# Attention and a SwiGLU block in one program: the same 1027 tasks, planned anew (order, engines, PSUM banks)

## The chip, the cores and the metric

The kernel runs on one core of a Trainium2 chip. That core has five engines with an instruction queue each: PE (TensorE, the matmuls), ACT (ScalarE), DVE (VectorE), POOL (GpSimd) and SP (SyncE, which here only issues DMAs). Each queue runs in its written order, and an engine waits where the next instruction's inputs or its buffer are not ready. The metric is the device time of one execution in microseconds (us), as a median over runs.

## The reference

```python
# q, k, v: 4 batches x 8 heads x 768 tokens x 64
scores = np.matmul(q, k.T) / np.sqrt(64)
causal  = rel >= 0                              # rel = query position - key position
stream  = causal & (key < 4 | rel < 64)         # 4 sink tokens and a window of 64
mask    = causal for heads 0, 2 and 6, stream for the other five
a       = softmax(where(mask, scores, -1e9))
x       = (a @ v) laid out as 3072 tokens x 512
g, val  = x @ w_gate, x @ w_val                 # 512 -> 1536
out     = (g * sigmoid(g) * val) @ w_out        # 1536 -> 512, float32
```

## The kernel before

All matmuls are in fp16 with float32 sums in PSUM. The 3072 queries are cut into 24 **tiles** of 128; two neighbouring tiles are a **pair** (0 to 11), and four tiles a **group** (0 to 5) of 512 tokens, on which the feed-forward part works. Everything is written as 1027 named **tasks**, each with its inputs, the engines on which it may run, and the buffers it takes:

- `load q3`, `load k3`, `load x3` (x is v) and `load g0`, `v0`, `o0` (pieces of the three weight matrices): DMAs on SP, L342 to L355, into a ring of 14 raw buffers.
- `cq3`, `ck3`, `cx3.m.j`, `wc g0`: casts to fp16 on ACT, DVE or POOL (L205, L207, L211).
- q and k turned so that the head dimension lies on the partitions: for pairs 0 to 4 by PE (`trq`, `trk`, L448, evacuated by `evq`, `evk`), for pairs 5 to 11 by DMA transposes on SP (`dq5.0` and so on, L438).
- `sc8.1`: score matmuls of tile 8, unit 1 (L542). `ex8.1`: the exponential on ACT (L554). `mask8.1`: a product with a 0/1 mask on DVE or POOL (L562), for tiles from 4 on; earlier tiles have the mask added by matmuls. `val8.1`, `val8.0`: a @ v for odd and even heads (L572). `nm8`: the softmax division on DVE (L579, L580), which writes the tile of x.
- `sk`, `sv`: copies of the sink tokens' keys and values to where the window's blocks find them.
- x turned: for tiles 0 to 7 by PE (`xtr`, L596, and `xe`), from tile 8 on by a DMA transpose on SP (`xdma8`, L590).
- per group g and slice j of 128 of the 1536 columns: `gate` and `vals` on PE (both L734, four matmuls of 512 columns; group 0 has its first slices in halves, `gate0.3.256`), `tanh` on ACT (L740), `stt1` and `stt2` on DVE (L744, L751), which make silu(g)·val, the buffer `h`. `gate` and `vals` hold a PSUM bank each until `stt1` and `stt2` have read it.
- `out2.3.0` to `.2`: the out projection of group 2, tile 3 in thirds (L769); `oe2.3.0` its evacuation on ACT or DVE (L205, L207); `st2.3.0` its store, issued by SP or ACT (L787).
- 22 filler matmuls on an identity (L314) at the start: 10 in the task `warm`, 12 between other tasks.

PSUM has eight banks. `gv` and `o` buffers take one bank, `big` ones (scores, and a @ v) two. So the order of tasks on PE, and which bank each takes, decide what a matmul must wait for: its inputs, and the last reader of its bank.

The order is written out as tables. `ORDER` has two base-62 digits for each task's number, in the order in which instructions are issued; numbers from 3700 on are filler matmuls. `WAYS` has a digit for each task: which of its allowed engines. `SLOTS` has a digit for each buffer that a task takes: which place of the ring, or which bank.

```python
        for t, w in zip(self.tasks, WAYS):
            t.way = t.ways[int(w)]
...
        ENG[task().way].tensor_tensor(out=ev, in0=ev, in1=mm, op=ALU.mult)      # L562
...
        eng = nc.scalar if T_st[g, tt, x].way == "ACT" else nc.sync              # L786
        eng.dma_start(out=out[r0:r0 + 128, lo:hi], in_=o_sbs[g, tt][:, lo:hi])
...
    for number in P.order():
        if number < P.FILL:
            running.append(P.tasks[number])
            P.tasks[number].run()
        else:
            warm((number - P.FILL) % 16, (number - P.FILL) // 16)
```

Each engine runs its share of `ORDER` in that order. Work of later tiles is woven into the feed-forward part of earlier groups: scores of tile 19, for example, stand among the gates of group 3.

Of the kernel before, what the change touches and what calls it, by code (L numbers as in the profile page):

```python
# [13 lines left out]


ORDER = (
    "00070306090A0C01041K1L08xy1T1I1Jy01Q1R1o1p0D1U1SyH1w1V1W0B1x1q0h1f1r1y1X0n02xh1z2K1g1d2021221k1e"
    "1O2B1N0E232Q1P292C1M2R0g2L2S1h2A1Y1Z2G1i1a1t2T1s1u0m1v1j24251b2U2D262E2V2W0i1c2X2Z2F272h132a282c"
    "0G1m2I1n2d142l2J2r2m052o0l8r2Y912s2b2O8w2n2w940F2P8s928z8t2N8p938x0z8u2M8y0o0y8m908c958n118h1l8o"
    "0r8S108q8d8X8v8i8k168e8f8j0k8T8a8Y8U2p8V8g31968Z0J8l8W9B971F8b2q2e0H9C2f98392i9D309a0q2g3A9f9b3B"  # L20
    "172t9g9c2u0I362v9E1G372x0j3F3I3G9F9d1C9h3J0p9i3H383C9e3K3D9V0Q3j9j9Q3L3P3E329W0x343b9R9X3T33993c"
    "9S1D3U3r0P9A3M3i3N3s3V3W0u3Z3t3X9Y19353a3o3O9T3Q0t3p3Y1A9Z3u3x3v9G0w9U3q3y9L3w0M9H2j3R3z2y9M3d9I"
    "3e3S9N9O2k553f2z549J529P2H453g483h4E18404FA95141AdAA58A7ABAeATAf0sAC0vAU0O49AgAD0K15AO0LAVAhARAP"
    "0R4A1EAn53AQA4Ao1B0SASAJA51HAp12AM9K59AKAEA6AWA83m0VALAH3kAN3n9kAF3l4M9lAXAG4S9mAIAY9n4TAiAZ4N5U"
    "AsAa0N50Av4UAtAu4B424C4V6643Aw9p4JAj4D9q57469r449o4GAk9s4Q4H56Al4R4I4K4PAx0ZAm5b4ZAy4W4e4j9u4aAz"
    "5T479v4X4b4O9w0c4f4Y9t4p9x4u4L4q4c9z4v4rA05a4dA15Z4mA24s4g4h0U4tAq4i4kA34nAbAr4l4o5HAc5A5I5K0TB2"
    "0d5BB06E5C4w4xB19yB36o7E6lB44y6nB75L5XB54z5WB8655JB96CBCBA6B7o5QBDBBBE7G5MBtBFBG5d5j5g5k0YBv5e0b"
    "C30W5h5fBq5cBw5iCA5YBxBr0aBgCBBs6DBMBuBhCCByBiBNC0Bz5NBO5OCD5P6869BPC167CE5R5oBlC2C5C4Bm7CBWC65D"
    "BQ5EBjBnBUC7BX5F5VBZ6kBk5G5u5r5vBYBoBa5S5sC85wBp625lC95m6s5t6L5p5x6MBb6r5n5yBeBc5z0X60Bd5qBR63Bf"
    "CF61BS7IBHBTCGBVBI647DBJ6jCHCI7LBK7HBL6I6FCJ6N7K6JCoCK6G6K0fCL6p6O6HCp6SCMCq6qDXCNCj7JDYD8DZCk0e"  # L30
    "DaClD9DBDb73DA6t7470DCDN6u75DG79DOCy7pDP6P6QCz7wCr716RD1Cs6U72D06Y6d6ZDQD26eDD6a6TDR6V6vDE7SD66W"
    "DFD3DH6X6mCeD4CPD5CfD7CQCgCR76CS776w6x787AChCT6yCt6A7T7B7rCi6bCu7P7M7u6cCwCv7QCm7vCO7RDSCx6fCnDT"
    "6g7NCUDU6hCV7O6iCWCZCX7X7t7FCaCY6zCb7UCc7VB6DV7WCd7g7xDW7a7h7dE47bEL7e7cEJEM7fEOENE1EPEGE2EfE3E5"
    "EiEgEHEkEhEIDIElEKEBDJEmDLDKECEp7ZDMDcEDEqEj7YDdEr7lDeDhDf7i7jEn7k7m84Eo7y7n8581Di8B7zDj8280Dm83"
    "DnDkDo7q868E878HDr8IDs8F8JDt8KDu8M88898NEd8A8CEV8G8L8DEQEWEEEXER7sEYEFEsESEZ8O8PEtDw8QDzDx8RE6Dy"
    "E9DvE7EaE8EAETEbFJEcEeFsFKEUFEFtFLFWFuDpG2E0DqFTDgFiFUFFFHFVDlFXFlFjFnFkFmFqFoEuFpFrG3FMFGGAFIG7"
    "FNG4FYG8FxG9FZGBFbFyFaG0FcFRFzG5G1FOG6FvFPFgFwFQEvFSEwEzExF0EyFdGCFeF1FfFhF4F2F5F3F6F9FAFBGDFCGE"
    "FDF7GHGFF8GIGGGJGMGKGNGLGOGRGPGSGQGTGWGUGVGXGY"
)
WAYS = (  # L40
    "000000000000000000000000000000000000000000000000000000000000222202202222222202220100222201100000"
    "000000000000220020220220011011000000000000000100220222011000000000000001201000000000002001222221"
    "001001000001000000001010000000000000002201000010010000000000020000000000000020202222000000000000"
    "000001100010000000000012012200000000000001001000020220220000000100000000100001001000002200222020"
    "000000000000000001000000000000000200200000000100000010000000101110210000001000000001200000000000"
    "021020200200000010000000000020000001000000000000000000000000000000000000000000000000000000000000"
    "000000000000000000000000000000000000000001000010000000000000000000000000000000000000000000000000"
    "000000000000000100001100000000010000000000000000000000000000000000000000000000000000000000000001"
    "100001000000001000000000000000000000000000000000000000000000000000000000000000010000110001000010"
    "000000000000000000000000000000000000000000000000000000000000000000000000000000010000000000000000"  # L50
    "0000000000000000000000000000000000000000000000001000100001000001010"
)
SLOTS = (
    "010523746A20796974080CAB6C17B52493D18B8DA51C93B8452163D10106040102241611232063220254440040006220"
    "616201436425612211161624043604454120646214300622320400616445611240622523226261404460404562163226"
    "113612440602263216220446045226106560612261024342246160132543246012162406142236445612242206143605"
    "0023111440102212311231000040220111550227010245020E1113A11049001182013501026302102104125F1004B212"
    "4I3021G3111D1000H0001M4112C1020K2010L2120J1121N0110024000104502081005A11046310472024E51010001511"
    "1243311152025211109021000124000M1011K1000G1120J4105I5120H0121F4001D302280020C4000L2122B300112025"
    "1149401142003201221002260123N5022541137510033104A111101004E122012010115M3002D2004C1012G5000H1110"  # L60
    "L4011J2014K5123B2103I301080104F300112001"
)
DIGITS = "0123456789ABCDEFGHIJKLMNOPQRSTUVWXYZabcdefghijklmnopqrstuvwxyz"

# [820 lines left out]
```

## Time and profile before

| | |
|---|---|
| time, median of 3 runs | 252.2 us (251.61 to 252.58) |
| the profiled execution's own time | 250.21 us |
| its span in the profile | 248.3 us |
| PE busy | 240.2 us, 97% |
| DVE, ACT, POOL busy | 165.7, 140.1, 84.7 us |
| DMA moved | 40.69 MB, mean 164 GB/s |
| instructions | 5187 |

The span runs from the first to the last instruction that the profiler recorded on the core; 1.9 us of that execution's time lie around it. Busy is the time in which an engine has an instruction in work, which for PE includes matmuls that are issued and still wait. A row of the timeline gives start and length in us, engine, line, operation, and in square brackets how long the engine had been idle and what released it. `SPq` is SP's queue issuing a DMA, and `DMA xt<-xb` the transfer itself. In the rows by source line, three numbers with slashes are the shortest, the median and the longest instruction in ns.

### The profile page before, as it was taken

How to read it: one execution, taken by the hardware profiler on the slowest of the kernel's cores; microseconds unless marked ns; L12 is line 12 of the kernel's file. 1: busy time of each engine (PE TensorE's matmuls, PEld its weight loads, DVE VectorE, ACT ScalarE, POOL GpSimd, SP SyncE). 2: the span in 40 equal slices, each digit the busy share in tenths (PEclk: the TensorE clock that was granted, in tenths of full speed). 3: DMA queues.
4: the chain of work that ended last, by engine and by line, in shares of the span. 5: the costliest groups of instructions: out<-in, count | busy, mean ns of one | idle time of the engine just before them, and what ended most of it. 6: DMA issues, size and time to landing. Idle time of an engine off the chain costs nothing.

```text
span 248.3 us, 5187 instructions
## 1 busy us (share of the span) xinstructions
PE 240.2 (97%) x2010; PEld 126.3 (51%) x2010; DVE 165.7 (67%) x294; ACT 140.1 (56%) x219; POOL 84.7 (34%) x114
## 2 busy tenths in 40 slices
PE   7999999999999999899999999999999999999995
PEld 2667765654444564444544545544455544444443
DVE  2579899967988654299886787546843767873111
ACT  3699778887674665656855765444544634231120
POOL 7578968760343444910510092310034000000000
PEclk9999999999999999999999999999999999999999
DMA  6999999958999999992598312460110223001142
GB/s 190 357 334 340 362 343 346 346 188 252 295 220 203 208 233 296 234 231 36 87 192 192 91 35 66 104 173 0 22 24 0 24 65 127 0 3 42 42 153 100
DMA packets 66951, 40.69 MB, mean 164 GB/s; under 512 B 25328, under 2 KB 60400, under 8 KB 66928
## 3 DMA queue, kind: packets, MB, share of 16 engines
q1 hardware_dynamic: 65776, 38.35, 60.4%
q10 hardware_dynamic: 1152, 2.03, 2.2%
q8 instruction: 15, 0.25, 0.4%
q14 instruction: 8, 0.07, 0.1%
HBM read 28.31 MB, written 6.29 MB: 139 GB/s over the span
## 4 chain that ended last, share of the span: by engine, by line
PE 76%; DMA 8%; SPq 7%; DVE 4%; ACT 2%; issue 2%; POOL 0%; DVEq 0%; POOLq 0%; ACTq 0%
PE banks L734 43%; PE banks L769 18%; PE banks L542 6%; PE banks L572 4%; SPq L438 3%; PE banks L314 3%; DMA kT<-hq 2%; DMA raw<-in_q_dram 2%; SPq L347 2%; ACT e L554 2%; DMA xt<-xb 2%; DMA out_dram<-o_sb 2%; PE banks L448 1%; DVE e L562 1%; SPq L590 1%
## 5 line engine op out<-in xcount | busy, mean ns | idle before, releaser
L734 PE MATMUL banks<-xt,wv_sb 128*128 128x512 f16 (+1 forms) x304 | 70.5, 368 | 2.0 <-issue 0.7
L554 ACT ACTIVATE e<-banks 128x1024 f16<-128x1024 f32 (+2 forms) x68 | 58.2, 909 | 24.9 <-PE banks L542 17.6
L734 PE MATMUL banks<-xt,wg_sb 128*128 128x512 f16 (+1 forms) x304 | 69.3, 368 | 0.0
L740 ACT ACTIVATE sig<-banks 128x512 f32<-128x512 f32 (+1 forms) x76 | 43.1, 575 | 41.5 <-PE banks L734 36.5
L769 PE MATMUL banks<-wo_sb,h 128*128 128x512 f16 (+2 forms) x300 | 64.8, 371 | 0.0
L744 DVE SCALAR_TENSOR_TENSOR sil<-sig,banks 128x512 f32<-128x512 f32 (+1 forms) x76 | 49.1, 656 | 18.5 <-ACT sig L740 16.6
L751 DVE SCALAR_TENSOR_TENSOR h<-sil,banks 128x512 f16<-128x512 f32 (+1 forms) x76 | 48.8, 656 | 6.2 <-PE banks L734 3.5
L769 PEld LDWEIGHTS <-h 128*128 128x128 f16 x300 | 28.3, 98 | 32.4 <-issue 0.3
L734 PEld LDWEIGHTS <-wg_sb 128*128 128x128 f16 x304 | 28.8, 98 | 31.2 <-issue 0.6
L734 PEld LDWEIGHTS <-wv_sb 128*128 128x128 f16 x304 | 28.2, 97 | 31.3 <-issue 3.1
L562 POOL TENSOR_TENSOR e<-e,m 128x1024 f16<-128x1024 f16 (+1 forms) x12 | 22.6, 1882 | 33.9 <-ACT e L554 27.6
L562 DVE TENSOR_TENSOR e<-e,m 128x640 f16<-128x640 f16 (+1 forms) x26 | 20.6, 800 | 15.0 <-ACT e L554 14.8
L207 DVE COPY o_sb<-banks 128x512 f32<-128x512 f32 (+1 forms) x13 | 8.6, 658 | 24.5 <-PE banks L769 20.6
L207 POOL CAST vt<-raw 64x512 f16<-64x512 f32 x27 | 18.4, 683 | 18.3 <-DMA raw<-in_v_dram 15.0
L205 ACT COPY o_sb<-banks 128x512 f32<-128x512 f32 (+1 forms) x12 | 6.9, 577 | 26.7 <-PE banks L769 26.2
L542 PE MATMUL banks<-qT,kT 64*128 64x128 f16 x472 | 20.2, 217 | 1.1 <-ACT e L554 0.5
L207 POOL CAST hq<-raw 128x1024 f16<-128x1024 f32 (+1 forms) x16 | 15.8, 989 | 15.6 <-DMA raw<-in_q_dram 6.4
L542 PEld LDWEIGHTS <-kT 64*128 64x128 f16 x472 | 14.6, 94 | 11.3 <-issue 8.9
L572 PEld LDWEIGHTS <-e 128*128 128x128 f16 x472 | 16.7, 97 | 5.0 <-ACT vt L205 0.8
L572 PE MATMUL banks<-vt,e 128*128 128x65 f16 x472 | 18.2, 193 | 0.5 <-ACT vt L205 0.5
L580 DVE TENSOR_TENSOR xb<-banks,rc 128x512 f16<-128x512 f32 x24 | 16.6, 692 | 0.8
L207 POOL COPY vt<-vt 2x330 f16<-2x330 f16 x12 | 6.0, 497 | 26.3 <-PE banks L572 25.9
(41 smaller groups left out, 119.2 us busy)
## 6 DMA issues: line engine op xcount, KB each, us to landing
raw<-in_v_dram SPq DMA_DIRECT2D x12, 512.0 KB, 6.7
raw<-in_k_dram SPq DMA_DIRECT2D x8, 512.0 KB, 6.5
raw<-in_q_dram SPq DMA_DIRECT2D x8, 512.0 KB, 5.6
out_dram<-o_sb SPq DMA_DIRECT2D x16, 256.0 KB, 2.3
raw<-in_moe_w_gate_dram SPq DMA_DIRECT2D x6, 512.0 KB, 8.3
raw<-in_moe_w_val_dram SPq DMA_DIRECT2D x6, 512.0 KB, 8.8
raw<-in_moe_w_out_dram SPq DMA_DIRECT2D x6, 512.0 KB, 7.6
raw<-in_q_dram SPq DMA_DIRECT2D x8, 256.0 KB, 6.0
```

The source lines that it names most:

```text
L207: ENG[task.way].tensor_copy(out=dst, in_=src)
L314: nc.tensor.matmul(to, ident, ident.unsqueeze(1).to_broadcast([128, 4, 128]), start=True, stop=True)
L542: nc.tensor.matmul(sc[:, c:c + n, :], weights, moving, start=first, stop=last)
L554: nc.scalar.activation(out=to, in_=src, func=AF.Exp, scale=scale)
L562: ENG[task().way].tensor_tensor(out=ev, in0=ev, in1=mm, op=ALU.mult)
L572: nc.tensor.matmul(avs[t][:, odd, n * 66:n * 66 + 65], ee, vv, start=(m == 0), stop=(m == len(bl) - 1))
L580: nc.vector.tensor_tensor(out=xb.rearrange("p n o d -> p o n d"), in0=av[:, :, :, 0:64], in1=rc.to_broadcast([128, 2, 4, 64]), op=ALU.mult)
L734: nc.tensor.matmul(ps, wsb[:, kk, j * 128:(j + 1) * 128], xt[:, kk, c[0]:c[1]], start=(kk == 0), stop=(kk == 3))
L740: nc.scalar.activation(out=sg[g, j, c], in_=gs[g, j, c], func=AF.Tanh, scale=0.5)
L744: nc.vector.scalar_tensor_tensor(out=sl[g, j, c], in0=sg.pop((g, j, c)), scalar=1.0, op0=ALU.add, in1=gs.pop((g, j, c)), op1=ALU.mult)
L751: nc.vector.scalar_tensor_tensor(out=hs[g, j][:, c[0]:c[1]], in0=sl.pop((g, j, c)), scalar=0.5, op0=ALU.mult, in1=vs.pop((g, j, c)), op1=A ...
L769: nc.tensor.matmul(o_open[g, tt, x], hs[g, j][:, tt * 128:(tt + 1) * 128], wo_sb[:, j, lo:hi], start=(j == 0), stop=(j == NJ - 1))
```

## The change

Only the three tables differ; the functions, the tasks, their inputs and the buffers are the same. One row of each:

```diff
 ORDER = (
-    "00070306090A0C01041K1L08xy1T1I1Jy01Q1R1o1p0D1U1SyH1w1V1W0B1x1q0h1f1r1y1X0n02xh1z2K1g1d2021221k1e"
+    "060700041I1J0105090203xy1Q1R1K1Ly11T1S0A1q1r1o1pyG1w1x1U1V1W1f1g1X1z1d1e1k1y0C2K2Q20222321292A2B"
...
 WAYS = (
-    "001001000001000000001010000000000000002201000010010000000000020000000000000020202222000000000000"
+    "001001000000000000010000000000000000002222220000100010010000010000100100000120022221000000000000"
...
 SLOTS = (
-    "010523746A20796974080CAB6C17B52493D18B8DA51C93B8452163D10106040102241611232063220254440040006220"
+    "001523647D128675761AC208B3D615479AC08B8C950A940B3A3CD9401016140002240610320143421642520240016142"
...
```

Decoded, this is:

- **PE.** Order at the start, before: `trk0 trq0 trq1 sc0.0 sc1.1 trk1 sc1.0 sc2.0 sc3.1 trq2 sc3.0 val1.1 val0.1 val0.0 val1.0 trk2 val2.1 val2.0 xtr0 val3.1 val3.0 sc4.0 sc4.1 xtr2 sc4.2 xtr1 xtr3 sc5.0 sc5.2 sc5.1 gate0.2.256 …`; after: `trq0 trk0 trq1 sc0.0 sc1.1 trk1 sc1.0 trq2 sc2.0 sc3.0 sc3.1 val0.1 val0.0 val1.1 val1.0 val2.1 val2.0 xtr0 trk2 val3.1 val3.0 xtr1 sc4.0 sc4.1 xtr2 xtr3 gate0.3.0 gate0.2.0 gate0.3.256 gate0.2.256 sc5.1 sc4.2 …`. Later groups are reshuffled in the same way. Fillers beside `warm`: 12 before (4, 5, 2 and 1), 11 after (2, 5 and 4).
- **SP.** q0 is loaded before k0, x1 before k2. From `st0.0.0` to `xdma11`, before: `st0.0.0 dq6.0 x9 dk7.0 xdma8 x10 st0.1.0 xdma9 dq7.1 dq7.0 q8 st0.3.0 xdma10 x7 q11 dk8.1 st0.2.0 xdma11` (loads by their names alone); after: `st0.0.0 q8 x9 dk7.0 dq6.0 dq6.1 xdma8 dq5.1 dk6.0 dk6.1 st0.1.0 xdma9 k10 st0.3.0 dq7.1 xdma10 dq7.0 dk8.1 dk8.0 xdma11`.
- **Engines.** 114 tasks change theirs:

| tasks | moves |
|---|---|
| masks | 10 from DVE to POOL, 7 from POOL to DVE (POOL has 12 before, 15 after) |
| casts of v (`cx`) | 11 ACT to POOL, 7 POOL to DVE, 2 ACT to DVE, 3 others |
| casts of q and k | 4 ACT to POOL, 4 POOL to DVE, 7 others |
| output evacuations (`oe`) | 8 DVE to ACT, 6 ACT to DVE |
| stores (`st`) | 7 SP to ACT, 4 ACT to SP |
| sink copies (`sk`, `sv`) | 13 to POOL, 8 from POOL, 2 others |
| others (`ev`, `wc`, `xe`) | 11 |

- **Buffers and banks.** About 500 of the digits in `SLOTS` change, most of them PSUM banks.

Masks on POOL before: 6.1, 11.0, 13.0, 13.1, 14.0, 15.1, 15.0, 19.0, 18.0, 20.0, 22.0, 23.1. After: 4.1, 9.1, 9.0, 8.0, 8.1, 11.1, 13.0, 13.1, 12.0, 14.1, 14.0, 15.1, 20.0, 17.0, 21.1.

More of the change, by code (lines that the diff above doesn't have):

```diff
@@ L16 @@
 ORDER = (
-    "00070306090A0C01041K1L08xy1T1I1Jy01Q1R1o1p0D1U1SyH1w1V1W0B1x1q0h1f1r1y1X0n02xh1z2K1g1d2021221k1e"
[L18 to L36, printed above, removed]
@@ L37 @@
-    "FNG4FYG8FxG9FZGBFbFyFaG0FcFRFzG5G1FOG6FvFPFgFwFQEvFSEwEzExF0EyFdGCFeF1FfFhF4F2F5F3F6F9FAFBGDFCGE"
-    "FDF7GHGFF8GIGGGJGMGKGNGLGOGRGPGSGQGTGWGUGVGXGY"
+    "060700041I1J0105090203xy1Q1R1K1Ly11T1S0A1q1r1o1pyG1w1x1U1V1W1f1g1X1z1d1e1k1y0C2K2Q20222321292A2B"
+    "2G2C2R2S081N1P1O1M1Y1Z1a1h1i1j0B1v1t1s2425261b0D2L2T1u2D2E2F1c1m1n2U2W2V2X2Z2a2h27282I2J0h138w8x"
+    "8y8m8n8o9192938r8s2o2c2d0n148z8p948u908t951l8q8v0m118k2p2q0g0y8X0z8c8Y8Z8d8e8S8T8U2l2m2n2r2s8f8g"
+    "2b2Y8h8i8j8l0i169B9C9D9697108V8a8W8b980E2N2M2e2O2f2g2i0l1F9a9b9c9f9g2P2t2u2v0F303637380G31393A3B"
@@ new lines @@
+    "0r1G9d9e9h2w3F3C3G3H3D3E0o17999A9E9F3I3J3K3L0k1C9V9Q9W9X9R9S3P3b3Z3c3a0J3j3r3s3t9i9j2x0I3i3o3p3q"
+    "0H3533323M3N3O3Q3T3U3V3W3X3Y0j199G9H9I9L9M3x3u3v0q1D9T9U9N9Y9Z2H0u182j3R2k3S343d3e3f0s122y2z0p1A"
+    "9O9P9J3y3g454B4C4D4E4F48494A0v1B3hAEA9AAABAYAWATAgAFAGARAUAZ0N4R4Q0Q520t159KAVAdAeAOAXAJAfAhAPAQ"
+    "ASAsAtAuACAKAMAiADALANAjAkAHAIA4A5A60x1HAvAw0K3l3n0L0M4P0w1E0T5V5W5X3kA7A8Aq0SAnAoApAa0R5T0P4041"
+    "4N4U4V0O4M4S0V9k9l9m9p9n9q9o3w420U0Z5U5bAr505657AxAyAz3z434644474T5158599r9u9s9v9t9w4J4W4X4Y4c4Z"
@@ new lines @@
+    "4j4a4b4d9x9y9zA0A1A2AbAc3m4G4H4I4L4KB0B10bA34e4f554u4v4m4nAl5a4O4g4h4i4l4k4s4t4p4q4rB2B35Z5H5I5J"
+    "666E6D5K5L5M5AAmB4B7B5544o4w4x4y6l4z6m5B5C6n6oB6B8B9BABCBDBE5c5Q5g5h5i5d5e5j5k5f656BC80W6967BFBG"
+    "Bq535D5E5F5G5N5O5P5S5RBWBXBYBrBs0a7CCI0d7oBtBuC5C6C7C9CFCGCHCJBlBmBn0e7p7wBvBwBxBoBpBMBNBOCACBBy"
+    "BzCCBPBQ5o5x5u5v5r627J5y5s5t5wC0BHBIBJBKBL5l5m5n5q5pBZBaBjC1C27IBRBSBT0Y5Y5z606163CDCEBUBVBbBcBd"
+    "BgBhBiBkBeBf68C3C46L6M6F6G6H64DBCeCfCgCjCkClD8D9DADCDXDYCoCpCqCmCnDZ6I6S6J6K6N6O0X6j6p6qDaDbBBDI"
@@ new lines @@
+    "DJDKChCi6P6Q6R6TCyCzD0D1D26k6r6s737071797274756t6u6vCKCLCMCPCNCQ6w6x6y7D7K7L7S7T6C6d6e0f7rD3D4D5"
+    "DLDMCrCs0c7G7F7ED6D776777A787H7M7N7O6V6W7x7sCRCSCTCUCVCWCZCXCY6U6z6Y6Z6a7P7Q7R6b7u7vCaCbCcCd6ADS"
+    "DTDU7U6c7V7WDNDODP6X6f6g6h6iDQDRDG7X7a7g7h7d7l7e7f7b7cDDDEDFDHCtCuCvDVCwCxDW7BE6EfEaEbEkEcEnEOEi"
+    "E7E8EgEhEjCOELEMENEPDcDdElEmEoDeDhDfDiDjDg7Y7i7j7m7k7y7z8081828B83DkDmDnDoDpDqDr8M8N86878H8I7Z7n"
+    "DsDtDu84858K8E8JE17q888L898F8A8GEQERESEpETEU7tEGEHEIDvEBECEJEKED8C8O8P8Q8REVEdEeEqErEEEsE9E2EWEt"
@@ L39 @@
+    "E3DzEYEADlDwDx8DFTEXFWFUEZFVFXFnFoG7GAFpG8FEEFFdG9FFGBFHFGFIFeFfFgFhG0FxFyFvFzG1FiFjFbFODyE0FPFq"
+    "FsFkFtFJFrFuFwFKFLG2G3E4E5G4FlFmFYFZFaFcFRFMFNEuG5G6EvEwExEyEzF0F1F2F4F5F3F6F9FAFBFCF7F8FDFQFSGC"
+    "GDGEGFGGGHGIGJGKGMGLGNGOGPGRGSGQGTGUGWGVGXGY"
 )
 WAYS = (
-    "000000000000000000000000000000000000000000000000000000000000222202202222222202220100222201100000"
-    "000000000000220020220220011011000000000000000100220222011000000000000001201000000000002001222221"
-    "001001000001000000001010000000000000002201000010010000000000020000000000000020202222000000000000"
@@ L44 @@
[L44 to L48, printed above, removed]
@@ L49 @@
-    "100001000000001000000000000000000000000000000000000000000000000000000000000000010000110001000010"
-    "000000000000000000000000000000000000000000000000000000000000000000000000000000010000000000000000"
-    "0000000000000000000000000000000000000000000000001000100001000001010"
+    "000000000000000000000000000000000000000000000000000000000000202202202202222222220012221200000000"
+    "000010000000110010222220011011000000000000002200122222011000000001000000201000000000001100222221"
+    "001001000000000000010000000000000000002222220000100010010000010000100100000120022221000000000000"
@@ new lines @@
+    "000000100000010000000012211200000010000001001000000110112000000100100000210000001000001201021220"
+    "000000000000000002000100000000000222012000000000000000000000202200210000001000000002100000010000"
+    "011022221100000000000000000110000000000000000000000000000000000000000000000000000000000000000000"
+    "000000000000000000000000000000010000000000100000000000000000000000000000000000000000000000000000"
+    "000000000000000010001000010000100000000000000000000000000000000000000000000000000000000000000001"
@@ L52 @@
+    "100001000110000000000000000000000000000000000000000000000000000000000000000000011000000000000000"
+    "000000000000000000000000000000000000000000000000000000000000000010001000010000000000000000000000"
+    "0000000000000000000000000000000000000000000000001000010001100001010"
 )
 SLOTS = (
-    "010523746A20796974080CAB6C17B52493D18B8DA51C93B8452163D10106040102241611232063220254440040006220"
-    "616201436425612211161624043604454120646214300622320400616445611240622523226261404460404562163226"
@@ L56 @@
[L56 to L60, printed above, removed]
@@ L61 @@
-    "L4011J2014K5123B2103I301080104F300112001"
+    "001523647D128675761AC208B3D615479AC08B8C950A940B3A3CD9401016140002240610320143421642520240016142"
+    "406101646325421132340616244602402145634114212426465600634021623162244543416163222060412162164454"
+    "102426023602541646234406362456102061252340212060416462124544426116024426004412364406220224165614"
+    "0013102351112511031131210400000102121025401360020B1113A11128000390020411207201102102011J4004F111"
+    "0H2003G3021E3022C5112L0024D1001N4020K0023I2020M0112001121016301242112A31228001170101300240402350"
@@ L62 @@
+    "1039510110020B20232001102111111J2023G2105E4102M0011C0110L3100F0011K2124D1100I0025N1020H320110023"
+    "124M1114K310370120920230012160125A2001110133002544022840155300250011025E5002H1124N500225020D0022"
+    "G5022L1003C4002F0021J3010I5022B120011021"
 )
```

## The prediction

> **What bounds the kernel now.** First the page's busy rows and slices, for the engine that is never free:
>
> ```profile
> PE 240.2 (97%) x2010; PEld 126.3 (51%) x2010; DVE 165.7 (67%) x294; ACT 140.1 (56%) x219; POOL 84.7 (34%) x114
> PE   7999999999999999899999999999999999999995
> PEclk9999999999999999999999999999999999999999
> PE 76%; DMA 8%; SPq 7%; DVE 4%; ACT 2%; issue 2%; POOL 0%; DVEq 0%; POOLq 0%; ACTq 0%
> ```
>
> TensorE (PE) is busy almost throughout at a granted clock that never falls, so only PE's lost time can move. But 97% hides how much is lost: a matmul that waits counts as busy. So I gave each matmul its undisturbed spacing, start to start in the densest runs of the trace (512 columns 0.2165 us, 256 0.109, 128 0.056, 65 0.0295, a score pair 0.0275), and summed: 228.7 us of PE work. A task's **debt** is its real start less the PE work ordered ahead of it. The last out-projection matmuls start at 244.4 with 228.1 ahead: debt 16.3, the whole of what an order can win. It grows thus: first gate 6.3 (start 22.1), first of group 1 8.7 (53.2), of group 2 11.8 (100.4), of group 3 13.7 (129.5), of group 4 15.7 (166.2).
>
> Next PE's own timeline, for where it grows (the bracket is idle time before the row and its releaser):
>
> ```profile
> 20.49 0.27 PE L542 MATMUL banks<-qT,kT 64*128 64x128 f16 x3 [0.48 <-ACT e L554]
> 25.42 0.60 PE L734 MATMUL banks<-xt,wv_sb 128*128 128x256 f16 x4 [0.51 <-DVE sil L744]
> ...
> 79.39 0.68 PE L542 MATMUL banks<-qT,kT 64*128 64x128 f16 x18 [0.46 <-DMA kT<-hq]
> 100.41 0.81 PE L734 MATMUL banks<-xt,wv_sb 128*128 128x512 f16 x3 [0.68 <-issue]
> ...
> 166.25 1.02 PE L734 MATMUL banks<-xt,wv_sb 128*128 128x512 f16 x4 [0.61 <-DMA xt<-xb]
> ```
>
> The losses in full: 3.7 before the first transposes; 2.35 in waits up to 25.4 us (0.24, 0.63 at val2.1 for a cast of v, 0.16, 0.65 at sc4.2, 0.67 at vals0.2.256); 3.0 in five waits later (0.65, 0.84, 0.38, 0.31, 0.83), two of the large ones for transposed tiles: xdma11 landed at 100.32 and xdma18 at 166.11, 0.1 before their matmuls; 29 runs of score matmuls, each 0.22 in entering and leaving, 6.4; the rest 0.85.
>
> SP's own timeline shows why a tile can land late, and the chain of waits that it counts:
>
> ```profile
> 92.40 0.58 SPq L347 DMA_DIRECT2D raw<-in_q_dram  x1
> 93.02 2.33 SPq L438 DMA_TRANSPOSE kT<-hq  x1
> 95.39 0.58 SPq L787 DMA_DIRECT2D out_dram<-o_sb  x1
> 96.07 1.21 SPq L590 DMA_TRANSPOSE xt<-xb  x1
> ...
> 161.90 4.22 DMA xt<-xb
> 166.11 0.14 issue
> 166.25 11.38 PE banks L734 x52
> ```
>
> SP issues one thing after another, and its issuing is the resource: from st0.0.0 (78.1) to the end of xdma11 (97.3) it has 18 issues and no gap.
>
> **The change, part by part.** All arithmetic stays but one filler matmul of 512 columns: 228.5 us of PE work, worth 0.2. Both orders have 29 score runs, so that 6.4 stays. The end (oe5.3.1, the store and its landing, about 3.05) stays: the same narrow last piece, its store on ACT in both. What is left is the waits. I walked the five new queues by hand: each task starts when its engine is free, its inputs are ready and its buffer's last reader is done, with durations from this trace.
>
> *Start to the first gate.* k0, q0 and the first casts swap places, one load of 0.46 to 0.57 either way: nil. Moved: x1 is loaded ahead of k2, so val2.1 no longer waits (−0.63); sc4.2 is placed behind four gates of group 0 (−0.65); xtr1 and xtr3 move up. The gates now begin with 15.0 us of work ahead, not 15.9, at 20.5: debt 5.5, a gain of 0.8, less than the sum because xtr3's evacuation is then late. At vals0.2.256 (24.2, with 18.3 ahead) it is 5.9 against 6.9: gain 1.0.
>
> *22 to 53 us.* The gain is given back. A windows view of this stretch and the next but one (columns: window, length, PE, PEld, DVE, ACT, POOL, granted clock, DMA share, GB/s):
>
> ```profile
> 22.12:53.19 31.07, 30.56 (x359) 20.34 (x357) 29.39 (x59) 25.07 (x47) 24.40 (x30) 1.00 1.08 345
> 100.41:129.48 29.07, 28.69 (x240) 14.35 (x240) 23.78 (x38) 18.25 (x31) 10.66 (x11) 1.00 0.74 150
> ```
>
> DVE is at 95% in the first and the DMA engines are full, so weights land no earlier. In my walk PE waits for DVE about 0.5 (vals0.11.0 takes the bank of 0.9.0, freed by L744) and for ACT 0.4 (sc9.0 behind ex8.1), and group 1 starts at 53.1 with 44.5 ahead: debt 8.6, gain 0.1. ACT is relieved: 13 casts of v leave it (13×0.62 = 8.0) and one comes; 11 of them go to POOL (0.68 each), while seven go from POOL to DVE. Nobody on PE waits for POOL's share here: they are due later than POOL's row shows it free.
>
> *Group 1, 53 to 100.* The 0.65 at 79.4 goes: the score run is ordered later, after its dk5 landing. The price is on SP. dk6.0 and dk6.1 were issued at 55.1 and 66.3, dq5.1 at 71.3 and dq6.1 at 76.1; now all four, and dk8.0, lie between st0.0.0 and xdma11. That stretch has 20 issues, 14 of them transposes (was 9): 19.2 + 5×1.25 − 3×0.6 = 23.6 us. It starts at 74.4 by the walk (a gap less ahead of it), so xdma11 is issued from 96.8 and lands, at the median of 3.2 from issue, at about 99.9. PE wants it at 99.0. Bounds: landings take 2.4 to 4.4, which makes the wait 0.2 to 2.2; I take the median's 0.9, close to the 0.84 of before. Behind xdma11 on SP only dk7.1 and later loads wait, with cover of 10 us. Group 2 starts at 99.9, 88.9 ahead: debt 11.0 (8.6, six score runs at 0.22, 0.9, and 0.2 of small waits), gain 0.8.
>
> *Groups 2 and 3, 100 to 165.* xdma12 to 15 are behind fewer casts and the load of k9; xdma15 lands at about 125.5 for a want of 126.6. The two waits of 0.38 and 0.31 go, and only two score runs lie in this stretch where four did (they moved to both sides of it). Debt at group 3: 11.0 + 2×0.22 = 11.4 (126.6, 115.2 ahead), gain 2.3. Then dk9.1 (lands 136.4 to 137.6, behind load q9 and st1.1.0) is just in time for sc19.1 at 138, and xdma19, behind xdma17 which needs nm17 (159.6), lands 163.4 to 165.2 for a want of 164.5: a wait of 0 to 0.7; I take 0.1 (the middle, 164.3, would be none), against 0.83. With six score runs (1.3; before five) group 4 starts at 164.9, 152.1 ahead: debt 12.8, gain 2.9. *After it* nothing in either order waits; three score runs bring the debt to 13.5, with rounding 13.6.
>
> *Masks.* POOL's go from 12 to 15 (10 arrive, 7 leave), each 1.4 or 2.1 there against 0.5 to 0.7 on a free DVE:
>
> ```profile
> L562 DVE TENSOR_TENSOR e<-e,m x26: 483/693/1670, 22.3 to 193.5; 128x640 f16<-128x640 f16 x14, 128x1024 f16<-128x1024 f16 x12
> L562 POOL TENSOR_TENSOR e<-e,m x12: 1393/2122/2130, 38.0 to 189.6; 128x1024 f16<-128x1024 f16 x8, 128x640 f16<-128x640 f16 x4
> ```
>
> The trace shows DVE's masks at 0.69 (1024 columns) when POOL is idle and 1.03 on average beside POOL's work, up to 1.67, while L744 and L751 are at 0.68 either way. [...] That speaks against this change, which puts about five pairs of a tile's masks on the two engines together (15.0 with 15.1, 11.0 with 11.1, 20.1 with 20.0). By the row that is 5×0.34 = 1.7 us of DVE[...]. DVE has 33% free, so most is covered by its idle time after group 0; uncovered is mask15.0, ahead of oe1.3.0, whose bank vals2.4.0 takes with 0.6 to spare: nil by the row[...]. I take the row. Small waits that a walk cannot see cost 0.3, as they do now.
>
> Sum: 16.3 − 13.6 + 0.2 (filler) − 0.3 = **−2.6**. The profiled execution (250.21; span 248.33 and 1.9 around it) is 2.0 below the median 252.2; the same step on the median gives **249.6**.
>
> **The rivals.** *(a) Given back again.* What 22 to 53 us shows happens once more in group 2 or 3: DVE, [...] by seven more v casts, frees a bank late. For it: DVE is 82% busy at 100 to 129; against: none of the five late waits of now names DVE. It would leave 0.7 of 2.6, the new SP order's part: 251.5.
>
> *(b) Slower: SP's queue ahead of xdma11.* Issue times of dk transposes are not steady: 1.2 mostly, but dk6.1 took 2.57, dk8.1 2.33 and dk7.1 2.47, all between 66 and 108 us, with loads queued around them. If the five added ones take 2.4 and not 1.25, SP slips 5.75 and group 2 starts that much later, one for one, with PE idle: 249.6 + 5.2 = 254.8. It decides from a slip of 4 us on (2.6 to no gain, 1.3 to be seen). Against: only three of 14 were long.
>
> *(c) No change at all* is out: 114 tasks change engine.
>
> **Numbers.** 0.5% of the median is 1.26 us, what a measurement here can tell from no change. Main case 0.64, 248.2 to 251.0 (landings 2.4 to 4.4[...]). (a) 0.18, of which a third is still faster. (b) 0.18. So faster 0.70, same 0.12, slower 0.18. The range leaves out the upper half of (b): 247.5 to 254.2.
>
> **What would show it.** First gate near 20.5; group 1 near 53; group 2 at 99 to 101 with xdma11 landing right ahead; group 3 near 126.6; group 4 near 165; last matmuls near 242. PE's waits at L542 below 0.5 us. Wrong if group 2 starts past 102 behind SP (b), or if waits for DVE of over 0.5 stand at L734 after 100 us (a).

## The result, and the profile after

| | before | after |
|---|---|---|
| median of 22 runs each | 250.64 us (248.84 to 253.13) | 252.43 us (251.20 to 255.24) |
| ratio, 95% interval | | 1.0073 (1.0047 to 1.0099) |
| the profiled execution, its span | 250.21, 248.3 | 251.2, 249.3 |

The change made the kernel 0.7% slower; the forecast was 1.0% faster (249.6 on 252.2). The three runs of before that the forecast had lay 1.6 us above the median of its 22, so ratios are compared from here on. A ratio leaves out executions that took over 1.5% more than the fastest of their kernel.

The page of after, the rows that were shown of before:

```profile
PE 241.7 (97%) x2009; PEld 127.7 (51%) x2009; DVE 167.2 (67%) x293; ACT 131.3 (53%) x204; POOL 92.2 (37%) x130
PE   7999999999999889999999999999999999999994
PEclk9999999999999979999999999999999999999999
PE 86%; DVE 2%; DMA 1%; issue 1%; ACT 1%; DVEq 0%; SPq 0%; ACTq 0%
```

Two marks differ. PE has two slices at 8 (81 to 94 us) where before has one (99 to 106), and the clock, which never fell before, has a 7. The chain of waits has less of DMA and SP in it than before (1% against 15%), which by itself would look like an improvement. PE's waits by releaser (columns: total us, times, longest), and its own timeline there:

```profile
PE banks L542 <- DMA qT<-hq: 2.0, 1, 2.0
...
88.05 0.62 PE L542 MATMUL banks<-qT,kT 64*128 64x128 f16 x14 [1.95 <-DMA qT<-hq]
88.60 1.79 PE L734 MATMUL banks<-xt,wv_sb 128*128 128x512 f16 x4
```

One wait of 1.95, at sc11.3, for a transpose of q; it is the only one of over 0.3 us that this view has after the start. The four matmuls at 88.60 take 1.79 us where four such took 1.02 in the rows shown of before. The windows view of PE around it says why (window, length, busy, granted clock, DMA share, GB/s):

```profile
86.00:88.00 2.00, 0.10 (x3) 1.00 0.81 180
88.00:89.00 1.00, 0.95 (x16) 0.86 0.59 92
89.00:90.00 1.00, 1.00 (x4) 0.50 0.78 130
90.00:91.00 1.00, 1.00 (x16) 0.50 0.84 270
91.00:92.00 1.00, 1.00 (x22) 0.50 0.64 123
92.00:93.00 1.00, 1.00 (x15) 0.93 0.33 66
```

The clock is halved from 88.7 to 92.1 us: 0.14 + 3×0.50 + 0.07 = 1.7 us of PE's time, counted as busy. And SP's timeline shows why q's transpose came late:

```profile
73.71 0.57 SPq L347 DMA_DIRECT2D raw<-in_k_dram  x1
74.64 0.36 SPq L787 DMA_DIRECT2D out_dram<-o_sb  x1
75.04 0.42 SPq L347 DMA_DIRECT2D raw<-in_q_dram  x1
75.52 1.51 SPq L347 DMA_DIRECT2D raw<-in_v_dram  x1
77.14 3.84 SPq L438 DMA_TRANSPOSE kT<-hq  x1
81.07 2.53 SPq L438 DMA_TRANSPOSE qT<-hq  x2
83.71 1.21 SPq L590 DMA_TRANSPOSE xt<-xb  x1
84.96 1.42 SPq L438 DMA_TRANSPOSE qT<-hq  x1
```

Behind three loads within 2 us the issue of dk7.0 took 3.84 us; dq6.0, dq6.1, xdma8 and then dq5.1 (84.96, landed 88.0) queued behind it. In debt, as the prediction counts it (real start less PE work ahead), with e6, a repaired version that comes below (each cell has start, debt):

| first of | predicted | after | e6 |
|---|---|---|---|
| gates | 20.5, 5.5 | 20.4, 5.5 | 20.2, 5.2 |
| group 1 | 53.1, 8.6 | 53.0, 8.5 | 52.7, 8.3 |
| group 2 | 99.9, 11.0 | 102.7, 13.8 | 99.1, 10.2 |
| group 3 | 126.6, 11.4 | 130.0, 14.8 | 127.4, 12.2 |
| group 4 | 164.9, 12.8 | 168.5, 16.4 | 165.9, 13.8 |
| last matmuls | debt 13.6 | debt 17.2 | debt 14.6 |

Up to group 1 the walk held to 0.1 us. Between 85.8 and 92.4 the debt rises from 9.2 to 13.3, and the excess stays to the end.

### The profile page after: what moved, and what is told of

Same layout as the page of the kernel before. It is cut to its first block, busy times and chain, and to the rows that moved or that the text cites. A ratio compares the mean times of both kernels' runs of the same rounds, so it can differ in the third digit from the quotient of the medians.

```text
span 249.3 us, 5198 instructions
## 1 busy us (share of the span) xinstructions
PE 241.7 (97%) x2009; PEld 127.7 (51%) x2009; DVE 167.2 (67%) x293; ACT 131.3 (53%) x204; POOL 92.2 (37%) x130
## 4 chain that ended last, share of the span: by engine, by line
PE 86%; DVE 2%; DMA 1%; issue 1%; ACT 1%; DVEq 0%; SPq 0%; ACTq 0%
PE banks L734 48%; PE banks L769 25%; PE banks L542 6%; PE banks L572 5%; DMA qT<-hq 1%; PE banks L448 1%; ACT e L554 1%; PE banks L596 1%; DVE h L751 1%; DVE sil L744 0%; DVE xb L580 0%; DVE e L562 0%; DVE rc L579 0%; DVE o_sb L207 0%; ACT sig L740 0%
## 5 line engine op out<-in xcount | busy, mean ns | idle before, releaser
L744 DVE SCALAR_TENSOR_TENSOR sil<-sig,banks 128x512 f32<-128x512 f32 (+1 forms) x76 | 49.3, 657 | 16.5 <-ACT sig L740 13.6
L734 PEld LDWEIGHTS <-wv_sb 128*128 128x128 f16 x304 | 28.8, 98 | 31.2 <-issue 1.1
L562 POOL TENSOR_TENSOR e<-e,m 128x640 f16<-128x640 f16 (+1 forms) x15 | 26.4, 1768 | 12.0 <-ACT e L554 10.1
L562 DVE TENSOR_TENSOR e<-e,m 128x1024 f16<-128x1024 f16 (+1 forms) x23 | 17.2, 755 | 14.5 <-ACT e L554 14.3
L207 POOL CAST vt<-raw 64x512 f16<-64x512 f32 x31 | 19.8, 640 | 14.3 <-DMA raw<-in_v_dram 12.9
L207 POOL CAST hq<-raw 128x1024 f16<-128x1024 f32 (+1 forms) x16 | 15.8, 999 | 21.5 <-DMA raw<-in_q_dram 10.2
L207 POOL COPY vt<-vt 2x330 f16<-2x330 f16 x14 | 7.3, 519 | 37.4 <-PE banks L572 37.1
L572 PEld LDWEIGHTS <-e 128*128 128x128 f16 x472 | 17.8, 99 | 5.4 <-issue 1.1
L205 ACT COPY o_sb<-banks 128x512 f32<-128x512 f32 (+1 forms) x14 | 8.1, 581 | 22.2 <-PE banks L769 21.1
L572 PE MATMUL banks<-vt,e 128*128 128x65 f16 x472 | 18.9, 196 | 0.5 <-DVE xb L580 0.3
L207 DVE COPY o_sb<-banks 128x512 f32<-128x512 f32 (+1 forms) x11 | 7.2, 652 | 17.8 <-PE banks L769 12.2
```

The costliest lines, as they stand in the source:

```text
L205: nc.scalar.copy(out=dst, in_=src)
L207: ENG[task.way].tensor_copy(out=dst, in_=src)
L572: nc.tensor.matmul(avs[t][:, odd, n * 66:n * 66 + 65], ee, vv, start=(m == 0), stop=(m == len(bl) - 1))
L734: nc.tensor.matmul(ps, wsb[:, kk, j * 128:(j + 1) * 128], xt[:, kk, c[0]:c[1]], start=(kk == 0), stop=(kk == 3))
L744: nc.vector.scalar_tensor_tensor(out=sl[g, j, c], in0=sg.pop((g, j, c)), scalar=1.0, op0=ALU.add, in1=gs.pop((g, j, c)), op1=ALU.mult)
```

## The experiments

Each moves entries of the tables with lines added to `Plan.order()`, so line numbers of their profiles are higher by up to 40. A pair `(a, b)` puts task a directly behind task b:

```python
at = {t.name: x for x, t in enumerate(self.tasks)}
for name, ahead in (...pairs...):
    numbers.remove(at[name])
    numbers.insert(numbers.index(at[ahead]) + 1, at[name])
```

The theory: SP's queue between st0.0.0 and xdma11 is too full as a whole, and a late transfer costs PE its wait and then half the clock. Rivals: only dq5.1's place is wrong; the clock has a cause of its own; or the new engines and banks are what is slow.

**e1: after, dq5.1 early.**

```diff
+ ("dq5.1", "dq5.0")
```

> The changed kernel with one issue moved on SP: dq5.1 directly behind dq5.0 (at about 73.7 us instead of 85). Place theory: only dq5.1's place costs; PE's wait of 2.0 at sc11.3 and the low clock behind it (0.59 of full speed over 88 to 92 us, 1.6 us of work) both go, and the time falls by 3.7 against the changed kernel, to 0.992 of the kernel before. Queue theory: SP is full from 74.6 us to xdma11, and two more needs stand close behind: dk6.1 landed at 90.5 where sc13.0 would now want it at 88.7, xdma11 at 102.0 where vals2.9.0 would want it at 99.0. Then the wait only moves: new waits of about 1.8 at L542 and about 1 at L734, xdma11 landing within 1 us of 102, and a gain of 0 to 1 us: 1.003 to 1.007 of the kernel before.

Measured: 1.0073 (1.0046 to 1.0100), 252.7 us: no gain. Where its profiled execution (255.6 us) waits:

```profile
102.56 0.80 PE L548 MATMUL banks<-qT,kT 64*128 64x128 f16 x19 [2.10 <-DMA qT<-hq]
104.77 1.86 PE L740 MATMUL banks<-xt,wv_sb 128*128 128x512 f16 x4 [1.42 <-DMA xt<-xb]
```

The wait at 88 is gone; PE runs on to the next transfers of the same queue, dq7.0 and xdma11, waits 3.5 us there, and the clock falls there. The theory of dq5.1's place alone falls. The queue theory had it that the waits only move. It named sc13.0 for the first new one, and it was sc14.1; and xdma11, which it had within 1 us of 102, landed at 104.7 in this execution.

**e3: after, with nine fillers in the wait.**

```diff
+ numbers.insert(numbers.index(at["sc10.3"]) + 1, self.FILL + 16 * 2 + 9)
```

> The changed kernel with nine filler matmuls (1.95 us) ahead of sc11.3, in a bank that sc11.3 takes anyway: they fill the wait for dq5.1 and change nothing else. If the low clock at 88 to 92 us comes from PE's idling before it, the clock stays at 1.00, the time spent on 88 to 92 us falls by 1.6 us, of which up to 0.7 shows before xdma11's landing at 102.0 becomes the bound: 0.5 to 1.6 us faster than the changed kernel, 1.001 to 1.005 of the kernel before. If the low clock has another cause, it shows at 88 to 92 us as before, and the time is that of the changed kernel, or longer by what the fillers exceed the wait: 1.007 to 1.009.

Measured: 1.0100 (1.0041 to 1.0160), 253.94 us, no faster than after. But the windows view of PE in its profiled execution answers the question on the clock:

```profile
88.00:92.00 4.00, 4.00 (x63) 1.00 0.72 156
102.00:104.00 2.00, 0.00 (x0) 1.00 0.57 98
104.00:108.00 4.00, 3.63 (x17) 0.58 0.39 63
```

With PE kept busy the clock stays whole at 88 to 92, and it falls behind the next wait, for xdma11, instead. So here the half clock came behind PE's idling, and filling one hole only moves PE to the next. The expected gain of 0.5 to 1.6 did not come: xdma11 landed at 104.3 in this execution, not at 102.0. Four of the six timed executions had a clock of 0.998 or more (after: 4 of 22) and were no faster for it (251.5 to 254.0), which fits a time that SP's queue sets.

**e4: before, dq5.1 late.** One issue, the other way round.

```diff
+ ("dq5.1", "dk7.0")
```

> The kernel before with one issue moved on SP: dq5.1 behind dk7.0 (at about 80.6 us instead of 71.3). sc11.1 wants it at 82.5 and gets it at about 84.9. All issues between move up by 1.25, so the old wait of 0.65 at sc10.0 for dk5 goes. A wait of 2.4 at sc11.1 less 0.65 is +1.8; the wait of 0.84 at vals2.6.0 is absorbed by the later PE: +0.9. If idling also brings a low clock as in the changed kernel, +1.6 more: +2.5, or 1.010 of the kernel before with the clock below 1; without it 1.003 to 1.004 and a clock of 1.00.

Measured: 1.0053 (1.0028 to 1.0079). In its profile:

```profile
PE banks L548 <- DMA qT<-hq: 2.5, 1, 2.5
```

The wait is as worked out. The clock stayed at 1.00 in this profile, but the mean granted clock of the timed executions was 0.993 or less in 9 of 22, against 4 of 59 for before and 18 of 22 for after. So the price lies between the two expected (1.004 without a drop of the clock, 1.010 with): the drop comes in some executions only. The 13 at a whole clock have a median of 251.8 us, 1.004 of before, as worked out without a drop. 0.993 is what one halving as long as that in after's profile, 3.4 us, makes in a span of 249 (3.4×0.5/249 = 0.7%). A single issue of a DMA, 9 us later on SP, costs the kernel half a per cent.

**e2: after, SP's queue relieved.** POOL's, PE's, ACT's and DVE's orders stay.

```diff
+ ("mask8.0", "dk5.1"), ("mask8.1", "mask8.0"), ("ck6.None", "mask8.1"),
+ ("dk6.0", "load q6"), ("dk6.1", "dk6.0"), ("dq5.1", "dq5.0"),
+ ("dk8.0", "load x8"), ("load k10", "load x8")
```

> The changed kernel with SP's queue alone reordered: dk6.0 and dk6.1 (with ck6 and two masks moved in the order, so that POOL's own order stays) ahead of dq5.0, dq5.1 directly behind it, dk8.0 and the load of k10 behind the load of x8. Every other engine keeps its order. Queue theory: xdma11 lands at 98 to 100, no wait of over 0.5 us is left at L542 between 80 and 100, the clock stays at 1.00, the debt at group 2 is 9.5 to 11, and the time falls by 3 to 4.5 against the changed kernel: 0.989 to 0.995 of the kernel before. Rival (the loss is in the banks and engines of the new plan, DVE's and POOL's masks among them): the wait moves elsewhere and the ratio stays at 1.004 to 1.010.

Measured: 1.0021 (0.9998 to 1.0044), 251.39 us: 0.5% better than after, where 1.2 to 1.8% was expected. In its profile group 2 starts at 99.7 with debt 10.8, close to the 99.9 and 11.0 that were predicted of the change itself, and the clock is 1.00 (0.993 or less in 8 of the 22 timed executions). The rest is lost to new waits:

```profile
PE banks L747 <- DMA xt<-xb: 2.3, 2, 1.4
```

They are for xdma11 (0.9) and xdma15 (1.4); a third, of 0.7, is for a cast of v on POOL (L585, for POOL vt L220). xdma15, from SP's timeline:

```profile
123.01 0.57 SPq L360 DMA_DIRECT2D raw<-in_k_dram  x1
123.68 1.22 SPq L603 DMA_TRANSPOSE xt<-xb  x1
```

It landed at 128.8, 5.1 us after its issue, right behind k9's 512 KB.

**e5: e2, with xdma11 ahead of dk8.1 and xdma15 ahead of k9.**

```diff
+ ("dk8.1", "load k10"), ("load k9", "load q9")
```

> SP's queue relieved further: beside the moves of the run before (dk6.0, dk6.1, dq5.1 early, dk8.0 and the load of k10 late), dk8.1 goes behind xdma11 and the load of k9 behind xdma15. There, PE waited 1.08 for xdma11 (landed 99.6) and 1.58 for xdma15 (issued 123.7, landed 128.8 behind k9's 512 KB). Theory (the new plan's gain is there, but each tile of x comes late behind other traffic on SP's queue): xdma11 lands at 98.5 or before, xdma15 at 127 or before, both waits below 0.4, and the time falls by 1.5 to 2.7 against that run: 0.991 to 0.997 of the kernel before. Rival (the later stages cannot be faster: banks, DVE and POOL follow): new waits take their place and the ratio stays at 1.000 to 1.004.

Measured: 0.9993 (0.9973 to 1.0014), 250.57 us, between the two. xdma15, ahead of k9, lands 2.5 us after its issue (124.2 to 126.7). The waits for tiles of x fall from 2.3 to 0.3, and POOL's grows to 2.0 (L587, for POOL vt L222).

**e6: e5, and one cast earlier on POOL.** cx7.1.1 stood behind three casts that wait for loads, a mask and the sink copy sv2.2.

```diff
+ ("cx7.1.1", "cx8.0.0")
```

> As e5, and one cast of v, cx7.1.1, earlier on POOL (behind cx8.0.0, where POOL was idle, instead of behind sv2.2), which val15.1 waited 0.89 for at 121. If that wait is POOL's own order, 0.5 to 0.9 faster than e5 (sv2.2 still ends 0.5 before): 0.988 to 0.995 of the kernel before. If xdma15 bounds group 3 anyway, e5's time.

Measured: 0.9937 (0.9905 to 0.9970), 248.95 us, and only now is the new plan faster than the old one. That is 1.6 us less than e5, more than the 0.5 to 0.9 expected: in the profiles the wait fell by 0.8, and the clock, half for 3.4 us behind it in e5, stayed whole; e5 had a lower clock in 4 of 22 executions only, so a part of the 1.6 stays open. The 1.2 us that are left of the wait (at L588, for POOL vt L223) are for sv2.2.

**e9: e6, and sv2.2 on ACT.**

```diff
+ self.tasks[at["sv2.2"]].way = "ACT"
```

> As e6, with the sink copy sv2.2 on ACT instead of POOL. There POOL came to it at 119.9 us, behind three casts that wait for loads (q10, q11, k11) and mask15.1, and val15.0 waited 1.2 to 1.4 for it; ACT was idle from 116 to 119.7. val15.0 then waits for mask15.1 alone (120.0): 1 us faster than e6, 0.988 to 0.992 of the kernel before. If xdma15's landing bounds group 3 anyway, e6's time, 0.993.

Measured: 0.9890 (0.9843 to 0.9937), 248.68 us, the lowest ratio of all. No wait for POOL's sink copies is left; the intervals of e6 and e9 overlap, so the step between them is not shown by the times alone.

**e7, e10, e11: e6, with the moved masks back on their old engines.** All 17; the seven that the change took off POOL; the ten that it put on POOL.

```diff
+ self.tasks[at["mask6.1"]].way = "POOL"    # e7 and e10; also 11.0 15.0 18.0 19.0 22.0 23.1
+ self.tasks[at["mask4.1"]].way = "DVE"     # e7 and e11; also 8.0 8.1 9.0 9.1 11.1 12.0 14.1 17.0 21.1
```

> As e6, with all 17 moved masks on the engine that they had in the kernel before (POOL 12, DVE 26). If the new choice of engines for masks costs (POOL's 2.1 us ones late, DVE's held up beside them), this is faster than e6 by 0.5 to 2 us. If it saves DVE time that PE waits for, slower by 0.5 to 1.5. The prediction's row (1.7 us of DVE, covered) has it within 0.5 us of e6.

> As e6, with the seven masks that the change took from POOL to DVE put back on POOL (6.1, 11.0, 15.0, 18.0, 19.0, 22.0, 23.1; 22 on POOL in all). All 17 put back cost 35 us. If the cost is POOL's queue (a mask waits there for its exponential, and casts of weights and v behind it come late), most of it is here: 20 to 35 us slower than e6, with waits of PE for POOL's casts. If it is DVE's, under 5.

> As e6, with the ten masks that the change took from DVE to POOL put back on DVE (4.1, 8.0, 8.1, 9.0, 9.1, 11.1, 12.0, 14.1, 17.0, 21.1; 5 on POOL in all). The prediction had the masks' moves at nil: within 0.5 us of e6. If DVE's queue is what the change relieved (L744 and L751, which free PE's banks, stand behind a mask that waits for its exponential), 5 us or more slower.

Measured: e7 1.1401 (1.1358 to 1.1445), 285.9 us; e10 1.0898 (1.0814 to 1.0981), 274.0; e11 1.0449 (1.0365 to 1.0534), 262.8 (the last two of two executions each). Against e6 that is 37, 25 and 14 us. e7's expectation fell in all its branches; e10 and e11 came as their branches of a queue had it, and not as the prediction had it (nil). First the waits of e10 (PE's, then POOL's), then those of e11 (PE's, then DVE's):

```profile
PE banks L568 <- DMA qT<-hq: 5.6, 1, 5.6
PE banks L598 <- POOL e L588: 5.5, 2, 4.5
PE banks L760 <- POOL wv_sb L233: 4.2, 2, 3.9
...
POOL e L588 <- ACT e L580: 34.8, 12, 11.6
```

```profile
PE banks L763 <- DVE xt L236: 4.1, 1, 4.1
PE banks L601 <- DVE e L591: 3.9, 3, 2.0
...
DVE e L591 <- ACT e L583: 22.3, 19, 3.7
```

A mask on POOL waits for its exponential with casts queued behind it: of weights (wc v2, for vals0.4.0), and of k. ck10 came late behind mask19.0 and mask18.0, SP waited for it to issue dk10.0, dq8.1 stood behind that on SP, and sc17.3 waited 5.6 us for dq8.1, the longest wait of all (in e7 too). A mask on DVE has the evacuation of a tile of x behind it (xe7, for the first gate of group 1). A part is the clock: it was half for 27, 24 and 7 us in the profiles of e7, e10 and e11, which is up to 14, 12 and 3 us of their losses. So the new order is worth nothing on the old engines. The new engines in the old order were not tried, and nothing here speaks against the old choice in the old order.

**e8: before, with its own three SP waits repaired.**

```diff
+ ("load x5", "dk5.1"), ("dk8.1", "xdma11"), ("st0.2.0", "xdma11"), ("st2.2.0", "xdma18")
```

> The kernel before with SP's queue alone reordered at its three waits for DMAs: dk5.0 and dk5.1 ahead of the load of x5, xdma11 ahead of dk8.1 and st0.2.0, xdma18 ahead of st2.2.0. All other engines keep their order. If its waits of 0.65, 0.84 and 0.83 are SP's order alone, 1.5 to 2.3 faster: 0.991 to 0.994 of the kernel before. If PE would only wait for something else a little later, 0.998 to 1.000.

Measured: 1.0027 (0.9996 to 1.0058); the expected gain did not come. dk5.1 landed at 78.3 instead of 79.8, but x5, moved behind it, landed at 81.5 instead of 78.9. Its casts on POOL came later, and the sink copy sk1.4 queued behind them:

```profile
PE banks L551 <- POOL kT L216: 1.7, 1, 1.7
```

The load that was in the way had a reader of its own, one engine further.

## Why the prediction was wrong, point by point

- **Start to the first gate, and 22 to 53 us: right**, both to 0.1 us, with the gain of 0.8 given back as worked out.
- **Group 1: the step that failed is the length of SP's stretch ahead of xdma11.** The sum had 1.25 us for each added transpose and 23.6 in all. It took 26.1 (74.6 to 100.7), and the excess is nearly all in one issue, dk7.0's 3.84. The prediction saw that three issues were long (2.57, 2.33, 2.47) and that loads stood around them, but not the pattern: in before each of the three stands directly behind two or more loads in a row, and dk7.0, behind x9 alone, took 1.23:

```profile
79.94 0.58 SPq L347 DMA_DIRECT2D raw<-in_v_dram  x1
80.62 1.23 SPq L438 DMA_TRANSPOSE kT<-hq  x1
```

  The change puts q8 and x9 directly ahead of dk7.0. Over the 13 traces of this case, all 35 transposes issued directly behind two or more loads (SP idle for less than 0.5 us) took 2.0 to 4.1 us, and the other 537 have a median of 1.2, with 48 of them over 1.6.
- **The slip met a reader that the walk did not look at.** It followed only xdma11. sc11.3 reads dq5.1, was due at 86.0 and got it at 88.0: 2.15 of debt where the sum had none. But the missing reader is not the failure by itself. At the walk's own lengths dq5.1 is issued at 74.4 + 3×0.6 + 4×1.25 = 81.2 and lands, after the median of 3.2, at about 84.4, an estimate that leaves 1.6 to spare. e4, which issues dq5.1 late by its place, shows that such a wait costs half a per cent in the old kernel.
- **The clock was missing from the sum**: 1.7 us in the profile. The clock in the profile of before was whole to the end, so its trace could not show it. The half clock of after lasted 3.413 us, and in all 13 traces the clock changed only at whole multiples of that after its first rise (in after the rise is at 6.81, the fall 24 multiples later, at 88.73). Counted in stretches of 3.413 us from there, of those begun at full clock all 15 with 2.0 us or more of idle PE were followed by a half-clock one, three of the five with 1.6 to 2.0, and none with less. That fits after, where 1.95 us cost the clock, and e4's profile, where 2.5 did not: the one lay in a single stretch (85.3 to 88.7), the other in two (1.1 and 1.3). Most of the 1.7 is covered, though, as the next point has it: after's four executions at a whole clock have a median of 252.2 us, the other 18 one of 252.8.
- **xdma11 would have been late in any case.** It landed at 102.0, 2.1 later than walked, which by itself starts group 2 at about 102 (an estimate; nothing else was due later). PE, late from sc11.3 and the clock, came at 102.7, so that the two losses cover each other: group 2 is 2.8 late, not 2.15 + 1.7 + 2.1. For the same reason e1, without the first, gains nothing. Of the 3.6 us of debt above the forecast at the end, these 2.8 are explained; the other 0.8 arose in groups 2 and 3 with no wait of over 0.3 in the trace. The profiled execution of after is also its fastest, 1.2 below the median (before's: 0.4), and that difference is not in this account.
- **Groups 2 and 3: wrong too, hidden in after.** The walk had xdma15 at 125.5 "behind the load of k9"; in e2 it was issued at 123.7, took 5.1 us behind that load, beyond the bound of 4.4 taken from before, and landed at 128.8. And sv2.2 and cx7.1.1 on POOL, 0.7 to 2.0 us, were not walked at all: POOL's share was said to be due later than needed. After does not wait for them, as PE is 3.4 us late there (xdma15 landed at 129.8, 0.2 before PE came). So removing the first wait alone (e1) or the first stretch (e2) gives little.
- **Masks: nil was right for the plan as it stands, and the row averages very unequal cases.** In after, five masks on DVE beside a POOL mask took together 2.5 us more than on an idle POOL (0.49 and 0.69), of which 0.9 in mask5.1 beside weight casts; the row had 1.7. The traces show what each one took: a DVE mask that started while POOL was inside an instruction took longer by what was left of that instruction less 0.15 us (no longer, where under 0.15 us was left). In before, mask14.1 (1.26 left) took 1.11 more; in after, mask15.0 (0.77 left) 0.62, mask17.1 (0.67) 0.53, mask21.0 (0.58) 0.44. Over the 13 traces 135 of 145 such masks fit to 0.02 us; of the other ten, eight started within 0.004 us of POOL's instruction and lost nothing, and two met POOL's next one as well. In after, mask11.0 began 0.05 us ahead of mask11.1 and lost nothing, and POOL took 1.90 for mask11.1 instead of 1.39. PE waits for none of them. That masks may be moved for nothing is wrong by 4 to 14% (e7, e10, e11), since the order around them is part of their cost.
- **The rivals.** (b) is what happened, smaller: SP ahead of xdma11, with its long issues, and its sign, group 2 past 102, came (102.7). One issue was long, not five, and the slip was 2.5, not 5.75; it was to decide from 4 on, and 2.5 was enough, since dq5.1's reader and the clock were in neither sum. It had 0.18. (a), DVE giving the gain back, is not what happened: no wait for DVE of over 0.3 stands after 30 us.
- **The gain can be had.** With SP and POOL mended at nine places, and the order of PE as changed, the ratio is 0.989 to 0.994 (e9, e6), which the main case had at 0.990. What the prediction took for a property of the change is one of the change and a mended queue. Whether the old plan could be brought as far is not shown: it had one set of repairs (e8), the new one four in a row.

## What to carry to other kernels

When issues move on a queue, price each by what will stand directly ahead of it, not by the median (2.0 to 4.1 us here behind two or more loads, a median of 1.2 otherwise): the long ones in the trace of before show behind what they were long. Then list for each one who reads it and when, not only for the one that is latest: the first late reader shows, and the later ones hide behind it, so removing one wait shows the next. Take a transpose behind a load as landing after that load, as all 166 with a load still under way did here. In a plan for in-order engines the choice of engine belongs to the order: 17 masks moved to other engines in an unchanged order cost 14%.

## What the runs showed of the hardware

- **A wait of PE cost more than its length.** After 1.95 us of idling the granted clock was 0.50 for 3.4 us (after, 88.7 to 92.1), 1.7 us of PE's time; with fillers in the hole it stayed 1.00 (e3, 88 to 92). Counted in stretches of 3.413 us from the clock's first rise, 2.0 us or more of idling in one was followed by a half-clock one in 15 of 15 cases; 2.5 us that lay in two stretches was not (e4's profile).
- **SP's issue of a transpose took longer directly behind two or more loads.** dk7.0, behind q8 and x9, took 2.6 to 4.1 us in all ten traces of the new order; in the three of the old, with x9 alone directly ahead of it, 1.2 to 1.3.
- **Transposes landed behind the loads issued ahead of them.** xdma15 landed 3.7 to 5.1 us after its issue behind a load of 512 KB (after, e1, e2, e3), and 2.4 to 3.0 ahead of it (e5, e6, e7, e9, e10, e11). In all 13 traces no transpose landed before a load that had been issued ahead of it: of the 166 with such a load still under way 1 us after their issue, each landed 0.4 to 3.2 us after it.
- **A DVE mask that started inside a POOL instruction took longer by the rest of that instruction, less 0.15 us** (1.26 left: 1.11 longer; 135 of 145 such masks to 0.02 us). Started 0.05 us ahead of a POOL mask, one took no longer than alone, and the POOL mask took 1.90 us instead of 1.39 (mask11.0 and mask11.1 in after).
